# Attention with mixture of experts on one core: the row sums and placement counts of a batch join the matmul group of its logits, high parts of the first rows are rounded by transfers, and the last copy stays on one engine

## The chip, the core and the metric

The kernel runs on one core of one Trainium2 chip. Its engines work in parallel, each through its own instruction stream in order: TensorE (PE, matmuls into PSUM), VectorE (DVE), ScalarE (ACT), GpSimd (POOL, which here mostly issues transfers) and SyncE (SP, which issues transfers). The metric is the device time of one execution in microseconds; several executions are timed and the median is given. Lower is better.

## What is computed

```python
# q, k, v: (8 batches, 12 heads, 448 positions, 64), cap = 30
scores = (q @ k.T) / 8
scores = cap * tanh(scores / cap)
attn = softmax(scores)                  # over the last axis
x = (attn @ v), heads side by side      # 3584 rows of 768
logits = x @ w_gate                     # 8 experts
e = argmax(logits); gate = softmax(logits)[e]
out[row] = gate * (relu(x[row] @ w1[e]) @ w2[e])   # w1: 768x1024, w2: 1024x768
```

All in 32-bit floats. In the experts' part each operand is split into a high part, rounded to a shorter format (fp32r), and a low part, the rest; three products of such parts take the place of one.

## The kernel before

**Attention, steps 0 to 83.** A "quad" is four heads of one batch, so a batch has 3 quads and the whole has 24; a quad has 7 tiles of 64 key positions, and a step handles 2 tiles. The loop `for k in range(STEPS + 3)` writes the work of each step for all engines:

- PE computes the scores of both tiles into two PSUM tiles `sp` (`scores`, L244, 4 matmuls a tile). There are only two such buffers, so the scores of a step can be computed only once ScalarE has read those of the step before.
- ScalarE applies tanh to both (`tanh`, L262) and then, for the step before, the exponential (`expo`, L267).
- PE multiplies by the values, three steps behind (`pv`, L309), into tiles `po`; VectorE copies a finished quad out to `ot` (`outp`, L322) and sums the exponentials over the tiles (`adds`, L276) into `acc` and `p4`.

Other work is hung into the steps by a table, `at(step, place, function)`, and done by `do(k, place)`: place "act" stands in a step ahead of the exponential, "pe1" after the value products, "v" at the end. For batch b, with n the step in which its last scores are computed, the table says: row sums of quads 0 and 1 on PE (`strips0`, L341) in step n + 1; logits and the row sums of quad 2 on PE (`strips`, L349) in step d = n + 5; then VectorE transposes and normalises (`rec_t`, `rec_v`), PE rearranges (`rec_p`, `log_p`, step p = d + 4), VectorE picks the expert (`route_v`), PE counts the places of the tokens per expert (`place_p`, L473, step p + 3), VectorE turns the counts into row numbers (`place_v`, step p + 4) and POOL scatters the token ids there (`place_d`, L500). Sums, logits and rearranged values share two PSUM buffers named `ms`; the counts stand in columns 256 to 295 of the rearranged values' tile.

**Early rows.** After batch 2 is placed, the busiest expert so far is found, and its first rows (block -2) are gathered to `xg`. In the last twenty steps VectorE scales a sixth of them (`scale_k`, L891), transposes it to `xt` (`trans_x`, L904; three buffers), ScalarE rounds the high part `xh` (`split_h`, L909), and VectorE subtracts for the low part `xl` (`split_l`, L913), one sixth every three steps. ScalarE also rounds the first chunk of this expert's first weights (`first_w1`, L825) in step 80, and VectorE subtracts.

**Experts.** From the end of the attention on, PE runs block after block: `up` (L926, first weights) and `down` (L949, second weights). The output of the last block is copied from PSUM in two halves of 384 columns, each followed by a scatter; the second half is split again, 192 columns by ScalarE and 192 by VectorE (L1299, L1300).

Of the kernel before, what the change touches and what calls it, by code (L numbers as in the profile page):

```python
# [15 lines left out]
B, H, S, D = 8, 12, 448, 64  # L16
NP = H // 2
DM = H * D
E = 8
# [6 lines left out]
NQ = NP // 2  # L26
QUADS = B * NQ
KT = S // 64
TILES = QUADS * KT
STEPS = TILES // 2  # L30
# [6 lines left out]
B_FIRST = 3  # L37
B_SECOND = 6
# [88 lines left out]
def attention_moe(tc, qT, kT, vL, capd, wgL, w1a, w1b, w2a, w2b, cst, cmk, out):  # L127
    nc = tc.nc
    V, A, G, PE = nc.vector, nc.scalar, nc.gpsimd, nc.tensor
# [25 lines left out]
    m = {"xp": xp}  # L155
# [3 lines left out]
    def load(mq, part):  # L159

        b, i = divmod(mq, NQ)
        p = slice(2 * i, 2 * i + 2)
        if part == 0:
            qr = raw.tile([128, 2, S], F32, name="qr")
            kr = raw.tile([128, 2, S], F32, name="kr")
            raws[mq] = qr, kr, pb.tile([128, KT, 2, D], F32, name="vr", bufs=3)
        qr, kr, vr = raws[mq]
        if mq == 0:
            if part == 0:
                nc.sync.dma_start(out=qr[:, 1], in_=qT[b, :, 1])  # L170
                nc.scalar.dma_start(out=qr[:, 0], in_=qT[b, :, 0])
                nc.sync.dma_start(out=kr[:, :, 0:128], in_=kT[b, :, p, 0:128])
                nc.scalar.dma_start(out=capt, in_=capd)
                nc.sync.dma_start(out=kr[:, :, 128:S], in_=kT[b, :, p, 128:S])
            else:
                nc.sync.dma_start(out=vr, in_=vL[b, :, i])
        elif part == 0:
            nc.sync.dma_start(out=kr, in_=kT[b, :, p])
            nc.sync.dma_start(out=qr, in_=qT[b, :, p])
        else:  # L180
            nc.sync.dma_start(out=vr, in_=vL[b, :, i])
# [14 lines left out]
    w1r = [rpool.tile([128, FC // 2, DM], F32, name=f"w1r{i}") for i in range(2)]  # L196
# [47 lines left out]
    def scores(t):  # L244

        m, g = divmod(t, KT)
        qr, kr, _ = raws[m]
        sp = sps[t] = ps_s.tile([128, 2, 512], F32, name="sp")
        for r in range(2):
            for c in range(2):  # L250
                h, w = slice(64 * r, 64 * r + 64), slice(64 * c, 64 * c + 64)
                PE.matmul(  # L252
                    sp[w, r, 0:S], kr[h, c, 64 * g : 64 * g + 64], qr[h, c, :], start=True, stop=True
                )
# [7 lines left out]
    def tanh(t):  # L262
        if t % 2 == 0:
            pts[t // 2] = pb.tile([128, 2, 2, S], F32, name="pt", bufs=5)
        A.activation(out=pts[t // 2][:, t % 2], in_=sps.pop(t)[:, :, 0:S], func=AF.Tanh, scale=qsc if t < KT else 1.0)  # L265

    def expo(k):  # L267
        A.activation(out=pts[k], in_=pts[k], func=AF.Exp, scale=capt)  # L268
# [35 lines left out]
    def fold(m):  # L304
        add(p4s[m], accs[m][:, 0], accs[m][:, 1])

    pvs, outs, yts, fin = {}, {}, {}, {}
# [14 lines left out]
    def outp(m):  # L322
        for c in range(2):
            ot = outs[2 * m + c] = op.tile([128, S], F32, name="ot", bufs=NP)
            V.tensor_copy(out=ot, in_=pvs[m][c][:, 0:S])  # L325
# [144 lines left out]
        for a in range(4):  # L470
            e.dma_start(out=xv[a], in_=yts[b][32 * a : 32 * a + 32])  # L471

    def place_p(b):  # L473

        pc = fin[b, "pp"].rearrange("p (q e) -> p q e", e=E)
        PE.matmul(pc, tri, ob, start=True, stop=False)
        for s in range(1, 5):
            PE.matmul(pc[:, s:5, :], ones, ob[:, 0 : 5 - s, :], start=False, stop=s == 4)
# [273 lines left out]
    def width(j):  # L752
        return LARGE if large(j) else SMALL
# [39 lines left out]
    w1s, w2s = [None] * FC, [None] * FC  # L793
# [9 lines left out]
    def high(i, f, e=A):  # L803
        w, r = ((w1s, w1r), (w2s, w2r))[i - 1]
        (e.copy if e is A else e.tensor_copy)(out=w[f][0], in_=r[f // 4][:, f % 4, :])

    def low(i, f, e=V):
        w, r = ((w1s, w1r), (w2s, w2r))[i - 1]
        hi, lo = w[f]
        e.tensor_tensor(out=lo, in0=r[f // 4][:, f % 4, :], in1=hi, op=ALU.subtract)  # L810

    def split_w1(f, e=V, eh=A):
        high(1, f, eh)
        low(1, f, e)
# [5 lines left out]
    def spare(name):  # L820
        return raw.tile([128, 2, S], F32, name=name).rearrange("p a b -> p (a b)").bitcast(F32R)

    def first_w1(f):
        w1s[f] = [spare(name)[:, 48 : 48 + DM] for name in ("qr", "kr")]
        split_w1(f)  # L825

    idt, gts = {}, {}

# [73 lines left out]
    xts = {}  # L902
# [5 lines left out]

    def split_h(j, k):  # L909
        n = width(j)  # L910
        A.copy(out=m["xh"][:, k, 0:n], in_=xts[j, k])  # L911

    def split_l(j, k):  # L913
        n = width(j)
# [110 lines left out]
    def at(step, when, f, *a):  # L1025
        tasks.setdefault((step, when), []).append((f, a))

    def do(step, when):
        for f, a in tasks.pop((step, when), []):
            f(*a)  # L1030

    for b in range(B):

        n = (KT * (b * NQ + NQ) - 1) // 2
        at(n + 1, "pe1", strips0, b)
        if b == B - 1:
            continue
        at(n + 4, "v", turn, b * NP + 4)
        at(n + 5, "v", turn, b * NP + 5)
        d = n + 5  # L1040
        at(d, "pe1", strips, b)
        at(d + 1, "v", rec_t, b)
        early = b < B - 2
        p = d + 4 if early else d + 5
        at(d + 2 if early else d + 3, "v", rec_v, b)
        at(p, "pe1", rec_p, b)
        at(p, "pe1", log_p, b)
        at(p + 1, "v", rec_c, b)
        at(p + 1, "v", route_v, b)
        at(p + 2, "act", route_s, b)  # L1050
        at(p + 2, "v", store, b, G)
        at(p + 2 if early else STEPS + 4, "v", route_g, b)
        at(p + 3, "pe1", place_p, b)
        at(p + 4, "v", place_v, b)
        for q in range(4):
            at(p + 5 + q // 2 * early, "v", place_d, b, q)
    for i in range(QUADS):
        if i % NQ != NQ - 1:
            n = (KT * (i + 1) - 1) // 2
# [15 lines left out]
    n = n_first + 19  # L1075
    at(n, "v", scale_c, -2)
    for k in range(KC):
        at(n + 3 * k, "v", scale_k, -2, k)
        at(n + 3 * k + 1, "v", trans_x, -2, k)
        at(n + 3 * k + 3, "act", split_h, -2, k)  # L1080
        at(n + 3 * k + 3, "v", split_l, -2, k)
    n_second = (KT * B_SECOND * NQ - 1) // 2 + 14
    at(n_second, "v", second_count)
    at(STEPS - 4, "act", first_w1, 0)
    at(STEPS + 1, "act", first_w1, 1)

    held = []
    for k in range(STEPS + 3):
        live = k < STEPS
        for n in range(QUADS - 3):  # L1090
            if k == (KT * (n + 1) - 1) // 2 + 1:
                load(n + 3, 0)
            if k == (KT * (n + 1) - 1) // 2 + 4:
                load(n + 3, 1)
        if live:
            for t in (2 * k, 2 * k + 1):
                scores(t)
                tanh(t)
        do(k, "act")
        if 1 <= k <= STEPS:  # L1100
            expo(k - 1)
        if k == STEPS:
            pools.close("ps_s")
            m["ps_h"] = pools("ps_h", bufs=2, space=PSUM, side="right", **tw)
            m["ps_z"] = pools("ps_z", space=PSUM, side="right", **tw)
            m["h0"] = spare("kr")
            up(-2, 0)
        last = None
        if k >= 3:
            ready = held + [2 * k - 6, 2 * k - 5]  # L1110
            held = [ready.pop()] if ready[-2] % KT == KT - 1 else []
            for t in ready:
                pv(t)
                if t % KT == KT - 1:
                    last = t // KT
        if last is not None:
            outp(last)
        do(k, "pe1")
        if 2 <= k < STEPS + 2:
            adds(k - 2)  # L1120
        if k == STEPS + 1:
            fold(QUADS - 1)
        do(k, "v")
# [12 lines left out]
    b = B - 1  # L1136
# [146 lines left out]
    for half in range(2):  # L1283
        V.tensor_scalar(
            out=o2[:, half : half + 1],
# [6 lines left out]
    for half in range(2):  # L1292
        for f in range(3, FC):
            down(j, f, range(1, 2), [half])
        src, dst = halved(j, 1, half)
        if half == 0:
            A.copy(out=dst, in_=src)
        else:
            A.copy(out=dst[:, :, 0:1], in_=src[:, :, 0:1])  # L1299
            V.tensor_copy(out=dst[:, :, 1:2], in_=src[:, :, 1:2])  # L1300
        scatter(
            out.rearrange("t (h x) -> (t h) x", h=2),
            o2[:, half : half + 1],
            ys[j][:, DM + 384 * half : DM + 384 * half + 384],
            2 * T - 1,
        )
    ys.pop(j)

    def value(t, bound, why):
        return nc.values_load(t, min_val=0, max_val=bound, skip_runtime_bounds_check_because=why)  # L1310

    more = value(tab["more"][0:1, :], 1, "zero or one")
    with tc.If(more > 0):
        for i, name in ((0, "large"), (1, "small")):
            cols = range(0, NL) if i == 0 else range(NL, NL + NS)
            cols = [c for c in cols if c not in ORDER]
            n = value(
                tab["nbi"][0:1, i : i + 1], (NL, NS)[i], f"the {name} blocks that hold a token, at most that many"
            )
# [69 lines left out]
```

## Time and profile before

| what | value |
|---|---|
| median of 3 runs | 783.78 us (783.6 to 784.56) |
| profiled execution | 782.08 us, of which the span of the trace is 780.1 us |
| PE | busy 765.6 us (98%) |
| DVE | busy 549.0 us (70%) |
| ACT | busy 451.3 us (58%) |
| POOL | busy 367.4 us (47%) |
| granted TensorE clock | 0.998 of full speed |

The profiled execution is 1.70 us under the median, and 1.98 us of it lie outside the trace's span. A matmul's end is modelled, so a busy PE need not be a PE at its fastest; the starts of instructions tell more. An instruction's busy time can also overlap that of the next one on the same engine, so the pace of an engine is read from start to start.

### The profile page before, as it was taken

To read this page: it belongs to the slowest core of one execution; us is meant where nothing else is said; L and a number is where in the kernel's file an instruction comes from. 1 tells how busy PE (TensorE), PEld (TensorE's weight loads), DVE (VectorE), ACT (ScalarE), POOL (GpSimd) and SP (SyncE) were. 2 spreads that over 40 slices of the span, in tenths; PEclk is the share of its full clock that TensorE was granted. 3 is DMA by queue.
4 is the path that set the end of the run, shared out by engine and by line. 5 is a ranking of instruction groups with operands and counts; after the bars stand their busy time and mean duration, and the time that the engine had idled before them with its cause. 6 is when DMAs were issued, how large, how long until landed. Compare 5 with 4: busy or idle time off the path is not lost.

```text
span 780.1 us, 14674 instructions
## 1 busy us (share of the span) xinstructions
PE 765.6 (98%) x5884; PEld 562.7 (72%) x5884; DVE 549.0 (70%) x952; ACT 451.3 (58%) x537; POOL 367.4 (47%) x323
## 2 busy tenths in 40 slices
PE   7999999999999999999999999999999999999995
PEld 3333343344343436999999999999999999999995
DVE  3788898999899998989458358357357367367820
ACT  7999999999999993335434324323333233234521
POOL 1001403035843210773774774774774774756601
PEclk9999999999999999999999999999999999999999
DMA  8436364457688230324264625525520226443401
GB/s 315 144 126 203 101 196 113 175 183 258 248 268 234 95 72 2 92 60 167 66 218 188 222 67 192 214 71 203 202 71 11 70 72 227 175 187 101 179 38 39
DMA packets 35276, 114.32 MB, mean 147 GB/s; under 512 B 8438, under 2 KB 14856, under 8 KB 32128
## 3 DMA queue, kind: packets, MB, share of 16 engines
q0 software_dynamic: 19264, 70.45, 27.4%
q1 hardware_dynamic: 15648, 42.62, 15.8%
q8 instruction: 48, 0.79, 0.4%
q14 instruction: 28, 0.23, 0.1%
q10 hardware_dynamic: 288, 0.23, 0.1%
HBM read 102.02 MB, written 24.22 MB: 162 GB/s over the span
## 4 chain that ended last, share of the span: by engine, by line
PE 64%; DVE 3%; ACT 2%; issue 0%; POOL 0%; POOLq 0%; DVEq 0%; ACTq 0%
PE ph L936 30%; PE y L966 22%; PE y L974 4%; PE po L318 2%; PE ms L966 1%; PE po L966 1%; PE z L966 1%; DVE acc L273 1%; PE sp L252 1%; ACT pt L268 1%; ACT pt L265 1%; PE ms L355 0%; DVE p L273 0%; DVE ot L325 0%; PE ms L347 0%
## 5 line engine op out<-in xcount | busy, mean ns | idle before, releaser
L946 ACT ACTIVATE hb<-ph 128x448 fp32r<-128x448 f32 (+1 forms) x67 | 33.9, 506 | 253.3 <-PE ph L936 253.3
L760 POOL DMA_INDIRECT xg<-xd,xi x114 | 135.0, 1184 | 55.7 <-issue 38.1
L268 ACT ACTIVATE pt<-pt,capt 128x1792 f32<-128x1792 f32 x84 | 154.4, 1840 | 0.0
L252 PE MATMUL sp<-qr,kr 64*64 64x448 f32 x1344 | 146.6, 545 | 4.4 <-ACT pt L265 3.8
L947 DVE SCALAR_TENSOR_TENSOR hb<-ph,hb 128x448 fp32r<-128x448 f32 (+1 forms) x67 | 38.0, 568 | 159.6 <-ACT hb L946 159.6
L318 PE MATMUL po<-pt,vr 64*64 64x448 f32 x1344 | 144.9, 537 | 0.6 <-DVE ot L325 0.6
L265 ACT ACTIVATE pt<-sp 128x896 f32<-128x896 f32 x161 | 141.8, 957 | 5.9 <-PE sp L252 5.6
L770 POOL DMA_INDIRECT out<-ys,xi x98 | 108.3, 1105 | 29.9 <-issue 27.7
L503 POOL DMA_INDIRECT ids<-tokg,slots x32 | 44.3, 1384 | 149.6 <-DVE slots L497 83.5
L318 PEld LDWEIGHTS po<-pt,vr 64*64 64x64 f32 x1344 | 56.5, 133 | 72.6 <-issue 62.4
L252 PEld LDWEIGHTS sp<-qr,kr 64*64 64x64 f32 x1344 | 47.7, 132 | 84.6 <-issue 39.2
L273 DVE TENSOR_TENSOR acc<-acc,pt 128x1792 f32<-128x1792 f32 (+1 forms) x36 | 61.1, 1698 | 2.6 <-ACT pt L268 2.5
L273 DVE TENSOR_TENSOR acc<-pt 128x896 f32<-128x896 f32 (+1 forms) x36 | 50.1, 1391 | 2.5 <-ACT pt L268 2.5
L911 ACT CAST xh<-xt 128x448 fp32r<-128x448 f32 (+1 forms) x54 | 27.4, 535 | 29.2 <-DVE xt L907 29.2
L325 DVE COPY ot<-po 128x448 f32<-128x448 f32 x48 | 27.6, 615 | 20.0 <-PE po L318 19.9
L936 PE MATMUL ph<-xh,qr 128*128 128x448 f32 (+1 forms) x108 | 37.2, 344 | 0.6 <-ACT pt L265 0.6
L936 PE MATMUL ph<-xh,kr 128*128 128x448 f32 (+1 forms) x108 | 37.2, 344 | 0.0
L936 PE MATMUL ph<-xl,qr 128*128 128x448 f32 (+1 forms) x108 | 37.1, 344 | 0.0
L471 POOL DMA_DIRECT2D xd<-w2r x12 | 8.1, 688 | 60.8 <-DVE w2r L336 60.3
L760 POOL DMA_INDIRECT w1r<-in_w1b,widx x7 | 9.5, 1352 | 47.5 <-DVE w17l L810 47.2
L907 DVE STREAM_TRANSPOSE xt<-xg 128x448 f32<-128x448 f32 (+1 forms) x54 | 30.3, 583 | 0.8
L915 DVE TENSOR_TENSOR xl<-xt,xh 128x448 fp32r<-128x448 f32 (+1 forms) x54 | 28.7, 556 | 0.0
(395 smaller groups left out, 1786.2 us busy)
## 6 DMA issues: line engine op xcount, KB each, us to landing
vr<-in_vL SPq DMA_DIRECT2D x24, 448.0 KB, 3.4
kr<-in_kT SPq DMA_DIRECT2D x23, 448.0 KB, 4.3
qr<-in_qT SPq DMA_DIRECT2D x23, 448.0 KB, 5.4
xd<-yt POOLq DMA_DIRECT2D x16, 336.0 KB, 5.1
xd<-w2r POOLq DMA_DIRECT2D x12, 336.0 KB, 3.9
xg<-xd,xi POOLq DMA_INDIRECT x114, 3.5
ids<-w1r SPq DMA_DIRECT2D x2, 882.0 KB, 7.3
out<-ys,xi POOLq DMA_INDIRECT x98, 2.3
```

The costliest lines, as they stand in the source:

```text
L252: PE.matmul(sp[w, r, 0:S], kr[h, c, 64 * g : 64 * g + 64], qr[h, c, :], start=True, stop=True)
L265: A.activation(out=pts[t // 2][:, t % 2], in_=sps.pop(t)[:, :, 0:S], func=AF.Tanh, scale=qsc if t < KT else 1.0)
L268: A.activation(out=pts[k], in_=pts[k], func=AF.Exp, scale=capt)
L273: V.tensor_tensor(out=o, in0=a, in1=b, op=ALU.add)
L318: PE.matmul(pvs[m][c][w, 0:S], vr[r, g, j, :], pt[r, j, :], start=g == 0, stop=g == KT - 1)
L503: i = G.indirect_dma_start(out=ids, out_offset=bass.IndirectOffsetOnAxis(ap=slots[0:p, c : c + 1].bitcast(U32), axis=0), in_=tokgs[b][0:p, ...
L760: G.indirect_dma_start(out=dst, out_offset=None, in_=src, in_offset=bass.IndirectOffsetOnAxis(ap=idx.bitcast(U32), axis=0), bounds_check=b ...
L770: i = G.indirect_dma_start(out=dst, out_offset=bass.IndirectOffsetOnAxis(ap=idx.bitcast(U32), axis=0), in_=src, in_offset=None, bounds_che ...
L936: PE.matmul(ph, w[:, 128 * k : 128 * k + 128], x[:, k, 0:n], start=i == 0, stop=i == 3 * KC - 1)
L946: A.activation(out=hh, in_=ph, func=AF.Relu)
L947: V.scalar_tensor_tensor(out=hl, in0=ph, scalar=0.0, in1=hh, op0=ALU.max, op1=ALU.subtract)
L966: PE.matmul(y[k][:, 0:LARGE], w[:, c], h, start=f == 0 and i == 0, stop=f == FC - 1 and i == 2)
```

## The change

The sums of quads 0 and 1 move from step n + 1 to step d, directly ahead of the logits, for batches 0 to 6. The counts (`place_p`) of batches 0, 1, 3 and 4 move to the end of the next batch's group of logits, a new place "pe2" in the step, and are written into free columns 448 to 487 of that batch's logits tile; `place_v` and the scatters follow them, some seven steps later than before. Batches 2 and 5 (after which the busiest experts are looked for) and 6 keep their counts where they were.

The six high parts `xh` of the early rows, and the high part of the first weight chunk, are no longer written by ScalarE but by transfers that POOL issues; the low parts follow one step later than before, that of the weights in step 81. The last copy is done by ScalarE alone.

```diff
-    def place_p(b):
-
+    def place_p(b, host=None):
+
+        if host is not None:
+            fin[b, "pp"] = fin[host, "log"][:, S : S + 5 * E]
         pc = fin[b, "pp"].rearrange("p (q e) -> p q e", e=E)
...
     def first_w1(f):
         w1s[f] = [spare(name)[:, 48 : 48 + DM] for name in ("qr", "kr")]
-        split_w1(f)
+        if f == 0:
+            G.dma_start(out=w1s[f][0], in_=w1r[0][:, f, :])
+        else:
+            split_w1(f)
...
     def split_h(j, k):
         n = width(j)
-        A.copy(out=m["xh"][:, k, 0:n], in_=xts[j, k])
+        if j == -2:
+            G.dma_start(out=m["xh"][:, k, 0:n], in_=xts[j, k])
+        else:
+            A.copy(out=m["xh"][:, k, 0:n], in_=xts[j, k])
...
-        at(n + 1, "pe1", strips0, b)
         if b == B - 1:
+            at(n + 1, "pe1", strips0, b)
             continue
...
+        at(d, "pe1", strips0, b)
         at(d, "pe1", strips, b)
...
-        at(p + 3, "pe1", place_p, b)
-        at(p + 4, "v", place_v, b)
+        o = 3
+        if b + 1 not in (B_FIRST, B_SECOND) and early:
+            o = (KT * (b * NQ + 2 * NQ) - 1) // 2 + 5 - p
+            at(p + o, "pe2", place_p, b, b + 1)
+        else:
+            at(p + o, "pe1", place_p, b)
+        at(p + o + 1, "v", place_v, b)
         for q in range(4):
-            at(p + 5 + q // 2 * early, "v", place_d, b, q)
+            at(p + o + 2 + q // 2 * early, "v", place_d, b, q)
...
-        at(n + 3 * k + 3, "act", split_h, -2, k)
-        at(n + 3 * k + 3, "v", split_l, -2, k)
+        at(n + 3 * k + 2, "v", split_h, -2, k)
+        at(n + 3 * k + 4, "v", split_l, -2, k)
...
-    at(STEPS - 4, "act", first_w1, 0)
+    at(STEPS - 6, "v", first_w1, 0)
+    at(STEPS - 3, "v", low, 1, 0)
...
         src, dst = halved(j, 1, half)
-        if half == 0:
-            A.copy(out=dst, in_=src)
-        else:
-            A.copy(out=dst[:, :, 0:1], in_=src[:, :, 0:1])
-            V.tensor_copy(out=dst[:, :, 1:2], in_=src[:, :, 1:2])
+        A.copy(out=dst, in_=src)
```

PE's stream before, around the logits of batch 0 (`sp` are scores, `po` value products, `ms` the logits with their sums; `p_` are the sums `p4`):

```order
L252 MATMUL sp<-qr,kr 64x448 x8
L318 MATMUL po<-pt,vr 64x448 x8
L355 MATMUL ms<-ot,wg 32x448 x3
L358 MATMUL ms<-p_405,cs 32x448
L355 MATMUL ms<-ot,wg 32x448 x3
L358 MATMUL ms<-p_405,cs 32x448
L252 MATMUL sp<-qr,kr 64x448 x8
```

and with the change:

```order
L252 MATMUL sp<-qr,kr 64x448 x8
L318 MATMUL po<-pt,vr 64x448 x8
L347 MATMUL ms<-p_211,cs 32x448
L347 MATMUL ms<-p_313,cs 32x448
L347 MATMUL ms<-p_211,cs 32x448
L347 MATMUL ms<-p_313,cs 32x448
L355 MATMUL ms<-ot,wg 32x448 x3
L358 MATMUL ms<-p_405,cs 32x448
L355 MATMUL ms<-ot,wg 32x448 x3
L358 MATMUL ms<-p_405,cs 32x448
L252 MATMUL sp<-qr,kr 64x448 x8
```

The four matmuls of L347 stood four steps earlier between a step's value products and the next scores; now 12 matmuls stand between them here instead of 8. In the groups of batches 1, 2, 4 and 5 the five short matmuls of the counts follow as well.

POOL's queue in the last twenty steps of the attention, with the change (`xd` are stores of attention rows, `ids` scatters of token ids, `xh` and `qr` the new transfers):

```order
L471 DMA xd<-w2r_124 32x14x192 x4
L917 DMA xh<-xt 128x448
L505 DMA ids<-tokg,slots 32256x14 x2
L917 DMA xh<-xt 128x448
L505 DMA ids<-tokg,slots 32256x14 x2
L917 DMA xh<-xt 128x448
L471 DMA xd<-yt 32x14x192 x4
L917 DMA xh<-xt 128x448
L505 DMA ids<-tokg,slots 32256x14 x4
L917 DMA xh<-xt 128x448
L828 DMA qr<-w1r_121 128x768
L917 DMA xh<-xt 128x448
```

Before, the same stretch held the stores and scatters alone; the new transfers stand between them, and each waits until those ahead of it have been issued.

## Rows read from the trace of the kernel before

**Rows 1.** Busy time by stage: PE, PEld, DVE, ACT, POOL in us (instructions); PEclk, DMA share, GB/s.
```profile
227.35:291.66 64.31, 62.62 (x729) 26.28 (x721) 61.44 (x101) 62.40 (x62) 17.08 (x16) 1.00 0.51 147
291.66:772.30 480.64, 480.57 (x2642) 448.42 (x2642) 299.22 (x551) 170.48 (x273) 286.96 (x250) 1.00 0.36 127
```
**Rows 2.** Chain that ended last: start, duration, work; its first piece in the experts.
```profile
291.66 3.88 PE ph L936 x18
```
**Rows 3.** Timeline of ACT around the logits of batch 0: start, duration, engine, line, work [idle before].
```profile
53.24 1.99 ACT L268 ACTIVATE pt<-pt,capt 128x1792 f32<-128x1792 f32 x1
54.91 1.93 ACT L265 ACTIVATE pt<-sp 128x896 f32<-128x896 f32 x2
56.51 2.02 ACT L268 ACTIVATE pt<-pt,capt 128x1792 f32<-128x1792 f32 x1
59.18 1.73 ACT L265 ACTIVATE pt<-sp 128x896 f32<-128x896 f32 x2 [0.66 <-PE sp L252]
```
**Rows 4.** Timeline of PE: sums of batch 0, a plain step, logits of batch 0.
```profile
41.25 1.68 PE L318 MATMUL po<-pt,vr 64*64 64x448 f32 x16
...
43.75 1.74 PE L252 MATMUL sp<-qr,kr 64*64 64x448 f32 x16
45.30 1.68 PE L318 MATMUL po<-pt,vr 64*64 64x448 f32 x16
46.81 1.68 PE L252 MATMUL sp<-qr,kr 64*64 64x448 f32 x16
...
54.88 1.68 PE L318 MATMUL po<-pt,vr 64*64 64x448 f32 x16
...
58.13 1.74 PE L252 MATMUL sp<-qr,kr 64*64 64x448 f32 x16
```
**Rows 5.** Timeline of PE: counts of batch 1 and sums of batch 2 in one group.
```profile
112.85 1.68 PE L318 MATMUL po<-pt,vr 64*64 64x448 f32 x16
...
115.56 1.74 PE L252 MATMUL sp<-qr,kr 64*64 64x448 f32 x16
```
**Rows 6.** Timeline of ACT: after sums, after counts with sums, after the last logits.
```profile
77.27 1.89 ACT L268 ACTIVATE pt<-pt,capt 128x1792 f32<-128x1792 f32 x1
79.22 1.73 ACT L265 ACTIVATE pt<-sp 128x896 f32<-128x896 f32 x2
...
114.80 1.89 ACT L268 ACTIVATE pt<-pt,capt 128x1792 f32<-128x1792 f32 x1
116.61 1.73 ACT L265 ACTIVATE pt<-sp 128x896 f32<-128x896 f32 x2
...
273.39 1.84 ACT L268 ACTIVATE pt<-pt,capt 128x1792 f32<-128x1792 f32 x1
275.88 1.73 ACT L265 ACTIVATE pt<-sp 128x896 f32<-128x896 f32 x2 [0.65 <-PE sp L252]
```
**Rows 7.** Timeline of ACT: one of six roundings of early rows, and of first weights.
```profile
266.38 0.58 ACT L911 CAST xh<-xt 128x448 fp32r<-128x448 f32 x1
266.83 1.82 ACT L268 ACTIVATE pt<-pt,capt 128x1792 f32<-128x1792 f32 x1
...
281.23 0.85 ACT L805 CAST qr<-w1r 128x768 fp32r<-128x768 f32 x1
```
**Rows 8.** Waits of DVE from 227.35 to 291.66: total us, times, longest us.
```profile
DVE ot L325 <- PE po L318: 1.0, 1, 1.0
DVE kr L810 <- ACT qr L805: 0.7, 1, 0.7
```
**Rows 9.** Timeline of the last copy.
```profile
772.27 0.32 ACT L1299 COPY ys<-y 128x192 f32<-128x192 f32 x1 [2.12 <-PE y L974]
772.62 0.36 DVE L1300 COPY ys<-y 128x192 f32<-128x192 f32 x1 [4.87 <-ACT ys L1299]
```
**Rows 10.** Transfers from 60 to 290: issues, KB each, median us from issue to landing.
```profile
xd<-yt POOLq DMA_DIRECT2D x16, 336.0 KB, 5.1
w1r<-in_w1b SPq DMA_DIRECT2D x4, 384.0 KB, 8.9
```

More of the change, by code (lines that the diff above doesn't have):

```diff
@@ L1118, in attention_moe @@
         do(k, "pe1")
+        do(k, "pe2")
         if 2 <= k < STEPS + 2:
```

## The prediction

> **What bounds the kernel now.** I read the busy time by stage first, then the chain, then the timelines of ACT and PE side by side. From 291.66 on, PE is busy 480.57 of 480.64 us [rows 1] and the chain that ended last is one row of its matmuls, beginning with the first `up` at 291.66 [rows 2]. The change touches nothing in there but the last copy, so the time moves by as much as the attention ends earlier or later, plus that copy.
>
> In the attention, PE and ACT are both nearly full, and what counts is how they meet. ACT's exponential of a step takes 1.67 us, start to next start (53.24 to 54.91) [rows 3]. So ACT loses time when the next tanh starts more than 1.67 after an exponential. After the logits of batch 0 it starts 2.67 after (56.51 to 59.18), a loss of 1.00, and the row names PE's scores as what it waited for [rows 3]. The last such place, batch 6, loses 2.49 - 1.67 = 0.82 [rows 6]; all seven lie between 0.8 and 1.1.
>
> Why PE is late there: a plain set of 8 value products takes 1.51 (45.30 to 46.81). With the sums of batch 0 behind it, it is 2.50 until the next scores (41.25 to 43.75), so that group costs 0.99. With the logits it is 3.25 (54.88 to 58.13), so those cost 1.74 [rows 4]. The logits are 8 matmuls of the same kind and the sums 4, so the matmuls of the sums take 1.74 - 0.99 = 0.75, and 0.24 is left as the price of breaking off and coming back. Counts and sums in one group cost 2.71 - 1.51 = 1.20 [rows 5], so counts beside others cost 0.21.
>
> Now the losses against the groups. After 1.20 ACT starts 1.81 after its exponential, a loss of 0.14; after the sums and a lag left from the steps before, it loses 0.28 (77.27 to 79.22) [rows 6]; after 1.74 it loses 0.8 to 1.1. **A group of about 1.06 us is free; what is longer, and what PE brought along as lag, ACT loses microsecond for microsecond.** The reason is the pair of score buffers: PE can run ahead no further.
>
> **The change part by part.**
>
> *Sums into the logits' group, counts behind them.* The sums' own groups, 0.99 each, were for the most part within the free 1.06, so little returns where they leave. The group of the logits grows by 0.75, to 2.49, and where counts join, by 0.96, to 2.70.
> - Batch 0: no small loss went away, +0.75.
> - Batch 2 (with counts of batch 1): +0.96, less the 0.14 that goes: +0.82. Batch 4 alike; the loss near its sums was about 0.3, so +0.65.
> - Batches 1 and 3: their sums stood after a step with a half set of products held over, and PE's lag there cost 0.28 + 0.1 ahead of the logits, which goes away; part of the lag that reached the logits goes too. Before, each lost about 1.36 in all. Now four plain steps lie ahead of the group, and in each PE gains 0.27 on ACT (1.67 + 1.60 [rows 3] against two sets of 1.50), so I take it to arrive without lag: batch 1 loses 2.70 - 1.06 = 1.64, +0.3, and batch 3, without counts, 2.49 - 1.06 = 1.43, +0.1. If the old lag stays after all, 0.3 more each.
> - Sum for batches 0 to 4: **+2.6 us** (2.3 to 3.2).
>
> *The stretch from 227 to 292, batches 5 and 6.* By ACT alone: the longer groups cost some +0.4 (batch 5 like batch 1, batch 6: 0.82 + 0.75 against 0.82 and 0.5 near its sums). Six roundings leave, 0.45 each (266.38 to 266.83), and one of 0.85 less the 0.13 that neighbours overlap [rows 7]: 6 x 0.45 + 0.72 = 3.4 us. But DVE is busy 61.44 of the 64.31 us, and its named waits there are two, 1.0 for value products and 0.7 for the rounded weights [rows 8]. None of DVE's work leaves: the same scaling, transposes, subtractions and `place_v` (that of batch 4 only moves some steps back). So DVE lets the stretch shrink by no more than 1.7, and the 1.0 sits right at the logits of batch 6, where PE's group grows by 0.75 and makes it longer. I set -0.7 (the wait for the rounded weights goes) and +0.9 (that wait, and the one that the group of batch 5 makes, grow): **+0.2**, with ends of -1.7 and +1.5.
>
> *Transfers for the high parts.* No row shows a transfer within SBUF that rounds. The nearest are POOL's stores of 336 KB, 5.1 us to landing; the longest weight loads of 384 KB take 8.9 [rows 10]. A sixth of the rows is 224 KB; I take 5.1, since it is the same queue. From a transpose to its subtraction there are three steps, 3 x 3.27 = 9.8 us, so 0 on the path. If that cover were gone, the wait would be DVE's, which has none to spare (a rival below). The last low part comes one step later, in step 83; it is wanted by the 17th of the 18 matmuls at 291.66, over 3 us in, so 0, at worst 1.
>
> *POOL's queue.* Batch 3's scatters now stand before the last two gathers of early rows and wait for `place_v` of that batch. Scaling begins five steps on, 16 us, so 0. SP's queue is not touched.
>
> *Last copy.* ACT's half takes 0.32 and DVE's 0.36 starts only after it, 0.71 in all [rows 9]. ACT's copy of 384 columns lies between 0.32 and 0.64; middle 0.48: **-0.2** (-0.4 to -0.1).
>
> **Sum:** 2.6 + 0.2 - 0.2 = +2.6 us. On the profiled execution, 782.08 becomes 784.7, its span 782.7; that execution was 1.7 below the median, so on the median 783.78 becomes **786.4 us**. This forecast's own range: 2.3 - 1.7 - 0.4 and 3.2 + 1.5 - 0.1 are +0.2 and +4.6; both ends at once are unlikely, I keep +0.8 to +4.1, 784.6 to 787.9.
>
> **The rivals.**
>
> *PE sets the pace: faster.* Before, seven groups of sums (three with counts in them), three of counts alone and seven of logits break the products; after, nine groups are left. Eight breaks of 0.24 are 1.9 us of PE. For it: PE is busy 62.62 of 64.31 [rows 1]. If ACT only waits because PE has too much to do over a whole batch, all of this returns: 783.78 - 1.9 - 0.2 = 781.7. Against it: 0.99 was free and 1.74 was not, within the same batch [rows 3, 4], so the loss is one of bunching. It decides if a group of 2.49 costs ACT no more than the one of 1.74 did. The Trainium skill has a rule for this side: its page TensorEngine Tiling (Array Packing), section Key Properties, says that changing the tiling mode drains TensorE; fewer changes are then a gain. The trace agrees that a change costs something, 0.24, but that rule knows nothing of the score buffers. Chance 0.09.
>
> *ACT sets the pace to the end: no change.* If DVE follows after all, since its waits on ACT and PE hide slack, the stretch gives 0.4 - 3.4 = -3.0, and the sum is 2.6 - 3.0 - 0.2 = -0.6: 783.2. For it: ACT is busy 62.40 of 64.31 [rows 1]. Against it: DVE's 61.44 are work that stays. Chance 0.18.
>
> *The transfers are late: slower still.* If a rounding transfer lands like the weight loads, 8.9 us, then with 0.7 to issue it and two scatters ahead of it in POOL's queue it misses the 9.8. DVE stops by some 0.5 us for each of six pieces: +3, 789.4. The Trainium skill's page SBUF — State Buffer, section "A bandwidth-pool intuition that's wrong", gives 620 ns for a GpSimd-issued transfer alone and 3100 ns beside a VectorE copy, because the descriptors wait. An estimate by it would be 5.1 + 2.5 = 7.6 us, still inside 9.8; no row here shows such a transfer. Chance 0.11.
>
> **How the numbers follow.** The forecast has 0.62, so that with the late transfers slower holds 0.72 (a part of its low end is within the bound), faster 0.09 from PE's rival, and the rest, 0.19, is no change. A measurement of this kernel tells about 0.2%, 1.57 us, from nothing. The range leaves out PE's rival and the far half of the late transfers: 783.4 to 788.6.
>
> **What would show it.** In the changed profile: ACT's loss after the logits of batch 0 should be 1.7 to 1.8 instead of 1.00, with the scores named; those of batches 2 and 4 near 1.8; the small losses near the old places gone; the first tanh of the early-row stretch some 2.6 later. From there to the first `up` about 64.5 us, DVE still over 61 busy; if that stretch is near 61, ACT's rival holds. The new transfers should land in 4 to 6 us, and no subtraction should wait for them. The first `up` starts near 294.5. I am wrong if ACT's losses at the logits have not grown, or if the stretch shrinks by its 3 us.

## The result, and the profile after

The changed kernel takes **787.63 us** (786.93 to 789.28, 6 runs) against 782.98 us for the kernel before in the same comparison (781.97 to 784.56, 6 runs): a ratio of 1.0062, 95% interval 1.0045 to 1.0079. It is slower by some 4.7 us. Its profiled execution took 787.06 us, the span of its trace is 784.8 us.

By stage, the stretch of the early rows and the experts (columns as in [rows 1]):

```profile
230.91:295.26 64.35, 61.89 (x730) 27.24 (x722) 60.45 (x100) 58.82 (x55) 19.26 (x23) 1.00 0.54 158
295.26:776.92 481.66, 480.74 (x2642) 448.07 (x2642) 300.49 (x552) 170.59 (x273) 286.71 (x250) 1.00 0.37 128
```

The first stretch is as long as before (64.31) although ScalarE is busy for 3.6 us less; it begins, with VectorE's first work on the early rows, 3.56 later. ScalarE's tanh behind the sixty-fourth exponential starts 3.03 later (225.52 to 228.55), where some 2.6 was forecast. The second is 1.0 longer than the 480.64 of [rows 1], with the same PE work.

ScalarE's timeline after the logits of batches 0, 5 and 6 (start, duration, engine, line, work [idle before]):

```profile
56.84 2.01 ACT L268 ACTIVATE pt<-pt,capt 128x1792 f32<-128x1792 f32 x1
60.26 1.73 ACT L265 ACTIVATE pt<-sp 128x896 f32<-128x896 f32 x2 [1.41 <-PE sp L252]
...
237.33 1.79 ACT L268 ACTIVATE pt<-pt,capt 128x1792 f32<-128x1792 f32 x1
241.51 0.92 ACT L265 ACTIVATE pt<-sp 128x896 f32<-128x896 f32 x1 [2.39 <-PE sp L252]
...
277.16 1.79 ACT L268 ACTIVATE pt<-pt,capt 128x1792 f32<-128x1792 f32 x1
281.13 1.73 ACT L265 ACTIVATE pt<-sp 128x896 f32<-128x896 f32 x2 [2.18 <-PE sp L252]
```

After batch 0 the next tanh starts 3.42 after its exponential, a loss of 3.42 - 1.67 = 1.75 where [rows 3] had 1.00. After batch 5 the loss is 2.51, after batch 6 2.30, against 0.82 in [rows 6]. PE's timeline in the same place shows why:

```profile
55.21 1.68 PE L318 MATMUL po<-pt,vr 64*64 64x448 f32 x16
56.82 0.96 PE L347 MATMUL ms<-p,cs 128*32 128x448 f32 x8
...
59.21 1.73 PE L252 MATMUL sp<-qr,kr 64*64 64x448 f32 x16
```

From the value products to the next scores it takes 4.00 us; without the 1.51 of the products [rows 4] that is a group of 2.49, the length forecast to the hundredth.

At the change to the experts, PE's timeline, and VectorE's:

```profile
298.38 0.36 PE L944 MATMUL ph<-xh,qr 128*128 128x448 f32 x1
299.62 0.47 PE L944 MATMUL ph<-xl,qr 128*128 128x448 f32 x1 [0.88 <-DVE xl L923]
```

```profile
296.88 1.15 DVE L325 COPY ot<-po 128x448 f32<-128x448 f32 x2
297.95 1.08 DVE L273 TENSOR_TENSOR acc<-pt 128x896 f32<-128x896 f32 x1
298.95 0.61 DVE L923 TENSOR_TENSOR xl<-xt,xh 128x448 fp32r<-128x448 f32 x1
```

The 17th of the first 18 matmuls stands still for the last low part, which VectorE makes only behind the copies and the sum of step 83. In [rows 2] the 18 ran through. The last copy:

```profile
776.92 0.48 ACT L1312 COPY ys<-y 128x384 f32<-128x384 f32 x1 [2.12 <-PE y L982]
```

It takes 0.48 where the two halves of [rows 9] took 0.71 from the first start to the last end.

To say where the time went I divided each profiled execution at four marks: the start of the eleventh exponential, that of the sixty-fourth, the first `up`, and the start of the last copy. ScalarE's rows for the first two marks in the changed kernel:

```profile
43.74 1.95 ACT L268 ACTIVATE pt<-pt,capt 128x1792 f32<-128x1792 f32 x1
...
226.86 1.89 ACT L268 ACTIVATE pt<-pt,capt 128x1792 f32<-128x1792 f32 x1
```

| us | to the 11th | 11th to 64th | 64th to first `up` | `up` to last copy | last copy to end | span |
|---|---|---|---|---|---|---|
| before | 43.42 | 180.33 | 67.91 | 480.61 | 7.83 | 780.1 |
| changed | 43.74 | 183.12 | 68.40 | 481.66 | 7.88 | 784.8 |
| e1_sums | 44.18 | 182.08 | 69.63 | 480.60 | 7.81 | 784.3 |
| e2_transfers | 44.14 | 180.45 | 66.25 | 481.68 | 7.98 | 780.5 |
| e3_counts | 45.30 | 180.68 | 68.09 | 480.60 | 7.83 | 782.5 |
| e4_last_piece | 45.06 | 183.10 | 68.91 | 480.61 | 7.72 | 785.4 |
| g1_pieces | 44.11 | 180.36 | 66.71 | 480.60 | 7.82 | 779.6 |
| g2_sums_counts | 43.67 | 183.09 | 70.22 | 480.62 | 7.80 | 785.4 |
| g3_pool_low | 44.93 | 180.30 | 66.16 | 480.60 | 8.11 | 780.1 |
| g4_earlier | 46.12 | 180.39 | 67.30 | 480.61 | 8.28 | 782.7 |

Each row is one execution. Between kernels that do the same there, the second column repeats within 0.15 us and the fourth within 0.02; for the third no two kernels do the same, but single waits in it repeat (the loss at the logits of batch 5 is 1.55 in e2_transfers, g1_pieces, g3_pool_low and g4_earlier). The first and the last column move by up to 2.7 and 0.6 us for reasons that no edit explains. So the change costs 2.8 in the second column, 0.5 in the third and 1.05 in the fourth. The other 0.3 of the 4.7 between the two spans lies in the first column, where nothing was changed, and 0.05 in the last.

### The profile page after: what moved, and what is told of

Same layout as the page of the kernel before. It is cut to its first block, busy times and chain, and to the rows that moved or that the text cites. A ratio compares the mean times of both kernels' runs of the same rounds, so it can differ in the third digit from the quotient of the medians.

```text
span 784.8 us, 14681 instructions
## 1 busy us (share of the span) xinstructions
PE 766.2 (98%) x5884; PEld 566.7 (72%) x5884; DVE 548.9 (70%) x951; ACT 447.8 (57%) x530; POOL 369.1 (47%) x330
## 4 chain that ended last, share of the span: by engine, by line
PE 60%; DVE 5%; issue 4%; POOL 0%; POOLq 0%; DVEq 0%
PE ph L944 28%; PE y L974 22%; PE y L982 2%; PE po L318 2%; DVE acc L273 2%; PE ms L974 1%; PE po L974 1%; PE z L974 1%; PE sp L252 1%; DVE ot L325 1%; PE ms L355 1%; DVE p L273 1%; PE ms L347 0%; POOL out L772 0%; DVE xg L899 0%
## 5 line engine op out<-in xcount | busy, mean ns | idle before, releaser
L762 POOL DMA_INDIRECT xg<-xd,xi x114 | 132.6, 1163 | 56.5 <-issue 38.1
L268 ACT ACTIVATE pt<-pt,capt 128x1792 f32<-128x1792 f32 x84 | 156.2, 1862 | 0.0
L265 ACT ACTIVATE pt<-sp 128x896 f32<-128x896 f32 x161 | 143.8, 981 | 13.0 <-PE sp L252 12.9
L318 PE MATMUL po<-pt,vr 64*64 64x448 f32 x1344 | 147.3, 537 | 2.4 <-DVE ot L325 2.4
L318 PEld LDWEIGHTS po<-pt,vr 64*64 64x64 f32 x1344 | 59.2, 133 | 73.2 <-issue 58.0
L919 ACT CAST xh<-xt 128x448 fp32r<-128x448 f32 (+1 forms) x48 | 23.8, 527 | 29.2 <-DVE xt L912 29.2
```

Of the source, the lines that this page charges most:

```text
L318: PE.matmul(pvs[m][c][w, 0:S], vr[r, g, j, :], pt[r, j, :], start=g == 0, stop=g == KT - 1)
L762: G.indirect_dma_start(out=dst, out_offset=None, in_=src, in_offset=bass.IndirectOffsetOnAxis(ap=idx.bitcast(U32), axis=0), bounds_check=b ...
```

## The experiments

Theory: PE's groups cost ScalarE whatever goes beyond what the two score buffers can hide, so that gathering them costs more than it saves; the late low part costs the rest. First rival: PE's work as a whole sets the pace, and fewer breaks return time. The first four kernels take the change apart.

**e1_sums**: before, with only the sums moved.

```diff
-        at(n + 1, "pe1", strips0, b)
         if b == B - 1:
+            at(n + 1, "pe1", strips0, b)
             continue
...
+        at(d, "pe1", strips0, b)
         at(d, "pe1", strips, b)
```

> Only the sums of quads 0 and 1 move to the logits; counts, roundings and last copy are those of before. Theory of bunching (what PE must do in one go beyond about 1.06 us, ScalarE loses, because only two score buffers exist): the losses after the logits of batches 0, 2 and 4 grow by 0.75 to 1.6 to 1.75, those of batches 1 and 3 to about 1.45, some of the small losses near the old sums go; about 2 us by the start of the early rows, and 1 more in batches 5 and 6: 2.5 to 4 us slower than before. Rival, PE's total work sets the pace: four lone groups of sums vanish and three share no more with counts, four breaks of 0.24 us less, so 1.0 us faster than before.

Measured: 786.3 us, ratio 1.0041 (1.0027 to 1.0054), 2.9 us slower, within the 2.5 to 4 expected. PE breaks off its products four times less and the kernel is 0.4% slower. ScalarE after the logits of batches 0 and 1:

```profile
57.28 2.02 ACT L268 ACTIVATE pt<-pt,capt 128x1792 f32<-128x1792 f32 x1
60.71 1.73 ACT L265 ACTIVATE pt<-sp 128x896 f32<-128x896 f32 x2 [1.41 <-PE sp L252]
...
91.89 1.94 ACT L268 ACTIVATE pt<-pt,capt 128x1792 f32<-128x1792 f32 x1
94.97 1.73 ACT L265 ACTIVATE pt<-sp 128x896 f32<-128x896 f32 x2 [1.14 <-PE sp L252]
```

The losses are 1.76 and 1.41. The gathering costs; PE's rival falls.

**e2_transfers**: before, with only the transfers and the later low parts.

```diff
...
-        at(n + 3 * k + 3, "act", split_h, -2, k)
-        at(n + 3 * k + 3, "v", split_l, -2, k)
+        at(n + 3 * k + 2, "v", split_h, -2, k)
+        at(n + 3 * k + 4, "v", split_l, -2, k)
...
-    at(STEPS - 4, "act", first_w1, 0)
+    at(STEPS - 6, "v", first_w1, 0)
+    at(STEPS - 3, "v", low, 1, 0)
```

> Only the high parts of the early rows and of the first weight chunk go by transfers, with the low parts at their new steps; sums, counts and last copy are those of before. If ScalarE set the pace from 227 to 292 us, its 3.4 us of roundings would come back whole: 3.4 faster up to the first up matmul. If VectorE sets it (my theory), at most its two waits of 1.7 us come back, and the last low part, which stands behind a copy and a sum in VectorE's order, makes the first up matmuls wait about 0.9 us again: -1.5 to +0.5 us in all.

Measured: 783.24 us, ratio 0.9994 (0.9982 to 1.0005). ScalarE lost 3.4 us of work, the stretch shrank by 1.66, and the experts took 1.07 more, with the same wait of PE as in the changed kernel. The whole lies in the expected range, and the 1.66 within the "at most 1.7" that VectorE was to allow; g3_pool_low, below, shows that the reason for it was another. PE's row:

```profile
295.20 0.47 PE L942 MATMUL ph<-xl,qr 128*128 128x448 f32 x1 [0.88 <-DVE xl L921]
```

**e3_counts**: before, with only the counts moved.

```diff
...
-        at(p + 3, "pe1", place_p, b)
...
+        if b + 1 not in (B_FIRST, B_SECOND) and early:
...
+            at(p + o, "pe2", place_p, b, b + 1)
...
```

> Only the counts of batches 0, 1, 3 and 4 move behind the logits of the next batch, the sums stay where they were. Theory of bunching: the logits' group of batches 1, 2, 4 and 5 grows by 0.21 us, so four losses grow by about 0.2; two lone groups of counts vanish (their losses of 0.1 at batches 1 and 5) and two beside sums (0.14 and about 0.2): within 1 us of before. Rival, PE's total work: two breaks fewer, 0.5 us faster.

Measured: 783.76 us, ratio 1.0003 (0.999 to 1.0015); 0.35 more in the second column. By themselves the counts cost next to nothing: at batch 2 the loss behind the logits grows by 0.3 and the 0.14 beside the sums goes.

**e4_last_piece**: the changed kernel, but the last of the six pieces as before.

```diff
...
+        if k < KC - 1:
             at(n + 3 * k + 2, "v", split_h, -2, k)
             at(n + 3 * k + 4, "v", split_l, -2, k)
+        else:
+            at(n + 3 * k + 3, "act", split_h, -2, k)
+            at(n + 3 * k + 3, "v", split_l, -2, k)
```

> The changed kernel, but the last of the six pieces of early rows is rounded by ScalarE and subtracted by VectorE in the step and order of before. If the 0.88 us that the first up matmuls wait for the last low part is on the path, the time falls by 0.9 less the 0.45 that ScalarE gets back, if that is on the path too: 0.4 to 0.9 us faster than the changed kernel, with no wait for the low part. Rival: the wait only covers another one (value products, weights), then no difference.

Measured: 787.3 us, ratio 1.0046 (1.0031 to 1.006). The experts are back at 480.61, no matmul waits, and the rounding by ScalarE puts 0.5 back on the stretch. By the marks that is 0.54 us less than the changed kernel, in the expected 0.4 to 0.9; the medians differ by 0.33, which their intervals do not tell from nothing.

The parts, 1.75 and 0.35 in the second column, make 2.1 where the whole has 2.8. The next kernels ask for that, and for a version without the losses.

**g2_sums_counts**: before, with the edits of e1_sums and e3_counts together.

> The kernel before, with both the sums in the group of the logits and the counts behind them; no transfers, the old last copy. Theory (the small losses near the old places are given back only once, by the sums; the counts then cost their 0.2 in each of four groups in full): from the eleventh exponential to the sixty-fourth 183.1 us, 2.8 over before, and with the 1.7 that the sums cost in the stretch of the early rows the whole is 4 to 5 us slower, ratio 1.0050 to 1.0065. Rival (costs simply add, 1.75 and 0.35): 182.4 in that part, and 3.2 to 3.6 us slower, ratio 1.004 to 1.0046.

Measured: 788.52 us, ratio 1.0065 (1.0044 to 1.0085); 183.09 in the second column, so the two are not additive. The 183.1 expected was the changed kernel's own figure; that it comes without the transfers is what was tested. In the third column it has 70.22, 2.3 over the kernel before and 1.8 over the changed kernel. The losses at the logits of batches 0 to 4 are 1.75, 1.61, 1.91, 1.79 and 1.92, those of the changed kernel. The counts' 0.2 falls where nothing is free any more, and the small losses next to the sums can be returned only once. Batch 3, whose group has no counts, went from 1.41 to 1.8 as well. The rows show that PE arrives there later: its sums begin 0.37 before ScalarE's last exponential in e1_sums and 0.03 after it in g2_sums_counts, a lag of 0.4. First e1_sums, then g2_sums_counts:

```profile
163.62 0.96 PE L347 MATMUL ms<-p,cs 128*32 128x448 f32 x8
163.99 1.94 ACT L268 ACTIVATE pt<-pt,capt 128x1792 f32<-128x1792 f32 x1
...
163.88 1.94 ACT L268 ACTIVATE pt<-pt,capt 128x1792 f32<-128x1792 f32 x1
163.91 0.96 PE L347 MATMUL ms<-p,cs 128*32 128x448 f32 x8
```

Where this lag comes from is not explained.

**g1_pieces**: before, with the transfers for five of six pieces (the edit of e4_last_piece), that of the weights, and the new last copy.

> The kernel before, with the transfers for five of the six high parts and for that of the first weights, the last high part by ScalarE and subtracted in its old step, and the last copy by ScalarE alone; sums and counts stay in their old places. Theory (the stretch of the early rows gains some 1.2 to 1.7 us, and the 1.2 us lost before the second step of the experts is due to the late low part alone): 1.2 to 1.7 us less than before and 0.1 for the copy, ratio 0.998 to 0.9985; the first up to the end takes 488.3. Rival (the gain of the transfers is given back in the experts whichever engine rounds the last piece): ratio 0.9995 to 1.0005 and 489.5 from the first up to the end.

Measured: 782.45 us against 783.53, ratio 0.9985 (0.9975 to 0.9996). This beats the kernel before by 1.1 us and the changed one by some 5. The ratio is at the upper end of the one expected; in the stretch the gain is 1.2, and from the first `up` to the end it takes 488.42, the theory's 488.3 and not the rival's 489.5.

**g3_pool_low**: g1_pieces, with POOL subtracting five low parts.

```diff
-        V.tensor_tensor(out=m["xl"][:, k, 0:n], ...
+        e = G if j == -2 and k < KC - 1 else V
+        e.tensor_tensor(out=m["xl"][:, k, 0:n], ...
```

> As the run with five transfers, but the five subtractions for the low parts of those pieces are done by POOL instead of VectorE. Theory (VectorE keeps the stretch of the early rows from shrinking by all that ScalarE saves): five subtractions of 0.6 us leave VectorE, and the stretch from the sixty-fourth exponential to the first up shrinks by a further 1 to 1.7 us, to about 65; ratio 0.996 to 0.998. Rival (PE with its longer group at the logits of batch 6 and its value products sets that stretch, VectorE does not): the stretch stays within 0.4 us of the run with VectorE's subtractions. Second rival (POOL and VectorE share a way to SBUF, and POOL's subtractions slow VectorE's work): the stretch is longer than with VectorE's, ratio 1.000 or above.

Measured: 783.13 us, ratio 1.0004 (0.999 to 1.0017). VectorE has five subtractions (2.9 us) less and the stretch shrinks by 0.55, not by 1 to 1.7, and by more than the rival's 0.4: VectorE holds a part of it at most. The second rival falls, the stretch is not longer. POOL takes 1.88 us in the mean for what VectorE does in 0.58, its five between 1.13 and 2.99 (groups by line: busy, mean ns | idle before):

```profile
L922 POOL TENSOR_TENSOR xl<-xt,xh 128x448 fp32r<-128x448 f32 x5 | 9.4, 1884 | 9.4 <-DMA xh<-xt 9.4
```

**g4_earlier**: all six transfers, scaling to subtraction one step earlier.

```diff
-    n = n_first + 19
+    n = n_first + 18
```

> The kernel before with all six transfers, that of the first weights and the new last copy, but scaling, transposing, rounding and subtracting of the early rows all one step earlier, so that the last low part is made in step 82 as before. Theory (only the step of the last subtraction costs the 1.2 us in the experts): first up to end 488.3, and the whole 1.2 to 1.8 us less than before, ratio 0.9977 to 0.9985. Rival (it is the last transfer in POOL's queue, or VectorE's work at the change to the experts, that costs it, whatever the step): first up to end 489.2 or more, ratio 0.9992 to 1.0005.

Measured: 782.82 us, ratio 0.9992 (0.9982 to 1.0002). From the first `up` to the last copy 480.61: the 1.05 hung on the step alone. The mark that I had named, first `up` to the end, reads 488.89, between the two answers, because the last transfer took 0.45 longer behind the copy. The gain in the stretch is only 0.6 here, so the whole missed its 1.2 to 1.8 and the version is no better than g1_pieces. Why the stretch gained less was not tried.

What then holds the stretch? The remaining four kernels ran on other, disturbed chips, where the kernel before itself took 867.5 and 813.8 us, with a granted clock of 0.94 to 0.98 from the first `up` on. So only the stretch, in which it is 1.00, is read from them, and set against executions on the other chips.

**h1_pieces_more_pe, h2_before_more_pe**: g1_pieces and the kernel before, with four extra sets of scores.

```diff
...
                 scores(t)
+                if t in (139, 147, 153, 163):
+                    scores(t, True)
                 tanh(t)
```

> The run with five transfers, and in steps 69, 73, 76 and 81 PE computes the scores of the second tile twice (the same values into the same buffer): four times 0.77 us more for PE alone, 3.1 in all, each in a step without a group. Theory (with the transfers in, PE sets the pace of the early rows' stretch): the stretch from the sixty-fourth exponential to the first up grows by 2.2 to 3.1 us, to 69 or more, and all that the transfers had given is lost. Rival (ScalarE and VectorE still set it, a group of up to 1.06 us is free): it grows by less than 1.2.

> The kernel before with the same four additions to PE, 3.1 us. Theory (before, ScalarE with its roundings set the pace of that stretch in the steps without groups, and PE had room): the stretch grows by 0.8 to 2.0 us, at least 0.7 less than in the run with transfers and the same additions. Rival (PE set the pace before too, and the transfers' gain comes from elsewhere): it grows by 2.5 or more, as much as with the transfers.

Measured: stretches of 67.58 and 68.23, 0.9 over g1_pieces and 0.3 over before, for 3.1 us of PE. My theory for the first fell, its rival held: PE does not set the pace there step by step, work in a step without a group is mostly free. For the second 0.3 lies below both answers. ScalarE's wait at the logits of batch 5 is 0.5 shorter in this execution than in the kernel before, so a part of the 0.3 may be owed to the execution.

What remains are the waits at the groups. In the kernel before, ScalarE's timeline ahead of the logits of batch 5 reads:

```profile
233.78 0.57 ACT L911 CAST xh<-xt 128x448 fp32r<-128x448 f32 x1
234.24 1.80 ACT L268 ACTIVATE pt<-pt,capt 128x1792 f32<-128x1792 f32 x1
237.00 1.73 ACT L265 ACTIVATE pt<-sp 128x896 f32<-128x896 f32 x2 [0.96 <-PE sp L252]
```

and the three waits of g1_pieces in the stretch:

```profile
237.71 1.73 ACT L265 ACTIVATE pt<-sp 128x896 f32<-128x896 f32 x2 [1.42 <-PE sp L252]
...
262.20 1.73 ACT L265 ACTIVATE pt<-sp 128x896 f32<-128x896 f32 x2 [0.88 <-PE sp L252]
...
276.59 1.73 ACT L265 ACTIVATE pt<-sp 128x896 f32<-128x896 f32 x2 [1.10 <-PE sp L252]
```

The rounding at 233.78 takes 0.46, start to start; without it the wait behind it is 0.46 longer. The other two waits of the kernel before are 0.65 [rows 6] and

```profile
261.49 1.73 ACT L265 ACTIVATE pt<-sp 128x896 f32<-128x896 f32 x2 [0.29 <-PE sp L252]
```

so in g1_pieces the three are longer by 0.46, 0.59 and 0.45, together 1.50 of the 3.0 us of roundings that were taken away, and the stretch shrank by 1.2. New theory: of the roundings, the first four stand ahead of a wait for a group and only fill it.

**i1_late_two, i2_early_four**: transfers for the fifth piece and the weights alone, and for the first four pieces alone; the diff is of the first, the second has (0, 1, 2, 3) in it and the weights' high part by ScalarE.

```diff
...
+        if j == -2 and k in (4,):
+            G.dma_start(out=m["xh"][:, k, 0:n], in_=xts[j, k])
+        else:
             A.copy(out=m["xh"][:, k, 0:n], in_=xts[j, k])
...
```

> The kernel before, with transfers only for the fifth of the six high parts and for that of the first weights, and the last copy by ScalarE alone. Theory (the first four roundings stood ahead of a wait of ScalarE for PE's groups and filled it, so that taking them away only lengthens that wait; the two behind the last group are the ones that count): nearly all of the gain of the run with five transfers stays, 0.45 + 0.72 = 1.2 us: the stretch from the sixty-fourth exponential to the first up takes 66.6 to 67.0, ratio 0.998 to 0.999. Rival (each rounding taken from ScalarE is worth the same share, because VectorE or PE lets only a part through): the stretch takes 67.3 to 67.6, ratio 0.999 to 1.000.

> The complement: transfers only for the first four high parts, the last two and that of the first weights by ScalarE as before; the last copy by ScalarE alone. Theory: the four gave nothing but a longer wait, the stretch takes 67.6 to 67.9 as in the kernel before, ScalarE's losses after PE's groups grow to 1.5, 1.2 and 1.3 us, ratio 0.9993 to 1.0005. Rival (equal shares): the stretch takes 67.0 to 67.3, ratio 0.9985 to 0.9993.

Measured: stretches of 66.09 and 67.28 (medians of 813.72 and 816.05, ratios 0.998, 0.9945 to 1.0015, and 1.0045, 1.0012 to 1.0078). Two transfers give 1.2 us more than four others; the rival wanted the four to be ahead. Both stretches are under the levels expected, by 0.5 and 0.3, and the second taken alone lies in the rival's 67.0 to 67.3; what speaks for the theory is the order of the two and the waits. ScalarE's waits, first of i1_late_two, then of i2_early_four:

```profile
245.31 1.73 ACT L265 ACTIVATE pt<-sp 128x896 f32<-128x896 f32 x2 [0.39 <-PE sp L252]
269.80 1.73 ACT L265 ACTIVATE pt<-sp 128x896 f32<-128x896 f32 x2 [0.30 <-PE sp L252]
...
284.19 1.73 ACT L265 ACTIVATE pt<-sp 128x896 f32<-128x896 f32 x2 [0.28 <-PE sp L252]
```

```profile
242.62 1.96 ACT L265 ACTIVATE pt<-sp 128x896 f32<-128x896 f32 x2 [0.86 <-issue]
...
267.11 1.73 ACT L265 ACTIVATE pt<-sp 128x896 f32<-128x896 f32 x2 [0.89 <-PE sp L252]
281.50 1.73 ACT L265 ACTIVATE pt<-sp 128x896 f32<-128x896 f32 x2 [1.11 <-PE sp L252]
```

The second and third waits of i2_early_four are those of g1_pieces, so four transfers bought waits. The first is some 0.6 shorter in both than in the pair before and g1_pieces (0.39 for 0.96, 0.86 for 1.42), and with that put back both stretches would be at the theory's levels; ahead of the stretch both show waits of up to 1.3 us named remote, which the undisturbed runs lack there, so that PE and ScalarE may have met otherwise; that was not tried. No run on an undisturbed chip confirms the stretches of this pair; the three longer waits of g1_pieces are from such a chip.

## Why the prediction was right, and where it was not

The forecast was 786.4 (784.6 to 787.9 by its own range, 783.4 to 788.6 in all) with 0.72 on slower; 787.63 is slower. That the time itself lies inside the narrower range is partly luck. The forecast was +2.6 (+0.8 to +4.1) on 783.78; the kernel before takes 782.98 in the comparison, and the difference is 4.65, beyond +4.1. What was right is the direction and the mechanism in batches 0 to 4; the parts:

- **Sums and counts, batches 0 to 4: +2.6 forecast, +2.8 measured.** Losses with what lies ahead of the logits, before and after: batch 0 1.00 and 1.75 (+0.75 forecast and found), batch 1 1.40 and 1.60 (+0.2 for +0.3), batch 2 0.97 and 1.90 (+0.9 for +0.8), batch 3 1.39 and 1.77 (+0.4 for +0.1), batch 4 1.15 and 1.90 (+0.75 for +0.65). A small loss near the sums of batch 5, 0.27, goes. One for one held where the same place is compared: at batch 0 the group grew by 0.75 and the loss by 0.75. The free 1.06 did not hold as a fixed length. It was read from one place [rows 5, 6], and [rows 3, 4] already gave 1.74 - 1.00 = 0.74 at batch 0, where it is 2.49 - 1.75 = 0.74 again. Batch 3 lost 1.77 and not the 1.43 of the rule; the prediction's "if the old lag stays after all, 0.3 more" is what came there. That two score buffers set the free length is argued from the kernel; no run changed their number.
- **PE's rival** fell by e1_sums. Of the rule in the Trainium skill's page TensorEngine Tiling (Array Packing), section Key Properties, that changing the tiling mode drains TensorE, the trace shows the price of 0.24; eight breaks fewer in the changed kernel, four in e1_sums, did not make up for the longer groups.
- **The stretch of the early rows: +0.2 forecast, +0.5 measured.** (In the window of [rows 1], which begins with VectorE's first row, 64.31 became 64.35.) The size is near by luck: two errors cancel. The longer groups alone, which the prediction's sum has at +0.9 (and at +0.4 by ScalarE alone, where its own terms for batches 5 and 6 add up to 0.55), cost 2.3 (g2_sums_counts, 70.22), and the transfers then give back 1.8, not 0.7. And the reason was wrong: "so DVE lets the stretch shrink by no more than 1.7" takes VectorE for the limit, but with five subtractions less on it the stretch shrank by 0.55 more only. ScalarE's rival, a stretch near 61, fell with 64.35. ScalarE's work falls by 3.4, and its losses from the sixty-fourth exponential on grow from 2.6 to 6.4: at batch 5's logits from 1.1 to 2.5, at batch 6's from 0.8 to 2.3. Part of that is the longer group, part the roundings that had filled the wait. g2_sums_counts has the longer groups and ScalarE's roundings, and its wait at batch 5's logits is 1.93, 0.46 under the changed kernel's 2.39:

```profile
237.71 1.80 ACT L268 ACTIVATE pt<-pt,capt 128x1792 f32<-128x1792 f32 x1
241.44 1.73 ACT L265 ACTIVATE pt<-sp 128x896 f32<-128x896 f32 x2 [1.93 <-PE sp L252]
```

  (In e2_transfers and g1_pieces, where the groups are the old ones, about half of the work taken away comes back as waits.) VectorE's wait for the value products grew as said, to 1.7 for the longer one, and that for the rounded weights is gone; it is busy for 60.45, a little under the 61 forecast:

```profile
DVE ot L325 <- PE po L318: 2.8, 2, 1.7
```

- **The late low part: 0 forecast, "at worst 1", measured 1.05.** This is the mis-sized term, and half of the 2.05 by which the difference went beyond the forecast. I had counted the 3 us until the 17th matmul and not VectorE's own work of step 83 ahead of the subtraction: two copies and a sum, so that it starts 3.69 us after the first `up` (295.26 to 298.95) and ends after 4.30. The matmul that follows starts 1.24 after the one ahead of it, in place of 0.2. The wait went away with the old step, whether ScalarE (e4_last_piece) or a transfer (g4_earlier) rounds the piece: both have 480.61.
- **Transfers: 5.1 to landing forecast, 5.8 measured; no subtraction waited for one.** The 5.8 is a single one: the trace holds the landing of one of the six. That no subtraction waited is read from VectorE's waits, whose one row, above, is for the value products. Rows of the transfers (issues, KB each, median us to landing):

```profile
xh<-xt POOLq DMA_DIRECT2D x6, 224.0 KB, 5.8
qr<-w1r POOLq DMA_DIRECT2D x1, 384.0 KB, 2.8
```

 The rival of late transfers falls. The estimate of 7.6 that I had made with the Trainium skill's page SBUF — State Buffer, section "A bandwidth-pool intuition that's wrong", was too long; VectorE was busy for 60.45 of 64.35 us beside these transfers. The moved counts, and the scatters with them, come three or four steps later (batch 0's in step 25 for 22), not seven as said ahead of the prediction.
- **The last copy: -0.2 forecast.** The copy itself is 0.23 shorter, as forecast; from its start to the end it takes 7.88 against 7.83, since the last transfer varies by more (7.72 to 8.28 over the runs). The gain can't be told from nothing.

## What to carry to other kernels

Where two engines meet over two buffers, price a group of foreign work by its length and by what the buffers hide: several short groups can be free where one long one is not, even if gathering them saves work. Before taking work from an engine, look for the next wait behind each piece: here the first four of seven roundings mostly filled waits, two carried the gain, and the last gave 0.5 and cost 1.05 behind it. And when a step is moved to the last moment, count what its engine has in front of it there.

## What the runs showed of the hardware

- A transfer within SBUF that rounds 224 KB landed in 5.8 us and holds POOL for 0.6 to issue it; that of 384 KB landed in 2.8. In the time of the first the DMA engines were full (share 1.02, 332 GB/s), in that of the second not (0.70). In g3_pool_low, where POOL's subtraction follows each transfer, 224 KB took 6.17 from issue to subtraction at a share of 1.00 and 2.33 at 0.53. So the time goes with the load of the engines rather than with the size; no run varied that load on purpose.
- POOL's subtraction of 128x448 takes 1.13 to 2.99 us (g3_pool_low, five of them), VectorE's 0.58 to 0.61.
- The time to the eleventh exponential moves by 2.7 us between the executions of the table (43.42 to 46.12), though nothing was changed there; that is more than most terms of this study; comparing stretches by their marks tells apart what the medians can't.
